# A fused attention, mixing and MLP block on one core: modulation sums in four column groups, V's low parts on another engine, later stores, and the mixing stage's first rows in a fixed buffer

## The chip, the core and the metric

The kernel runs on one core of a Trainium2 chip. The metric is device time in microseconds (us) of one execution, and lower is better. The engines named below are PE (TensorE: matmuls and transposes), DVE (VectorE), ACT (ScalarE), POOL (GpSimd) and SP (SyncE, which issues nearly all DMAs here). DRAM is the large memory outside the core. SBUF tiles live on 128 partitions, matmul results in eight PSUM banks of 128 x 512 fp32.

## The reference

One sequence of S = 2048 rows, D = 576 columns, F = 4608 hidden columns, 32 heads of 18 columns, everything fp32 in and out. The condition vector `c` (576) makes six vectors of 576 (shift, scale and gate for two branches). Cut to what matters:

```python
mod = silu(c) @ w_mod                     # six vectors: sa, ca, ga, sb, cb, gb
h   = layernorm(x) * (1 + ca) + sa
q, k, v = split(h @ wqkv)                 # 32 heads of 18
# every row attends to itself and the 255 rows before it
o   = softmax(q k^T * 18**-0.5, window 256) v @ wo
x   = x + ga * o
h   = layernorm(x) * (1 + cb) + sb        # the "hbd" rows
h2  = gelu(layernorm(h) @ w1)             # mixing: column groups shifted by +1, -1, +2, -2 rows
y   = h + shifted(h2) @ w2
z   = y + gelu(layernorm(y) @ w3) @ w4    # MLP
out = x + gb * z
```

## The kernel before

**Precision.** Nearly every 576-deep product is made of fp32r matmuls (a rounded fp32 format) on a high part and a low part of both operands, so that such a product of a 128-row by 512-column tile is 14 matmuls. Splitting an operand is a cast (high part) and a subtraction (low part), and the two run on ACT, POOL or DVE.

**Phase A** (`phase_a`, L189) is attention. Its work is a list `ev` of pairs (time, step). `play` sorts it and issues the steps in that order, and PE, DVE, ACT, POOL and SP keep the order in which they were issued. So the numbers in the list set the order of each engine, and each engine runs its row of instructions in order. The unit of time is a *unit*: 32 of them (four row blocks of 512 by eight groups of four heads), numbered 0 to 31. What happens before unit 0 has negative times and is called the head here.

**The head.** Some matmuls on zeros run first (`warm`, L264). `c_load` and `wm_load` bring `c` and the first third of `w_mod` (five pieces k = 0..4 of up to 128 rows by 1152 columns, L258). `cond` makes silu(c) and copies it to a tile `silub` of 128 x 640 in the ring of row buffers (tag "r", six of them). `mod_sum(k)` (L276) multiplies it by piece k with four fp32 matmuls of 128 rows by 256 or 320 columns, so that every PSUM partition holds the same sum; twenty instructions in all. `mod_col(j)` (L286) picks column j of the result to partitions by a multiplication with the identity, ten instructions on DVE. With `sa` and `ca` known, ACT makes `h` transposed (L373), POOL casts it to the high part of `hT` (L376), DVE makes the low part (L380). Then come the projections of block 0 (L391): an *item* is 14 matmuls, items 0, 4, 5, 1, 6, ... for Q and K (operand `Wc`), two per 128 rows for V (operand `Wv`). `Wv` is split per piece k: high part on ACT (L330), low part on POOL (L334).

**Packing.** Q and K go to DRAM and come back in the layout that the scores need: `pack(u)` (L457) issues twelve DMAs (L467 for Q, L469 for K) from SP. `scores(u)` (L483) takes 128-row maxima, `attend(u)` makes the scores again with the maxima subtracted (L530, L539), exponentials on ACT (L549, tile `P`), the products with V (L560, four column groups of 32), a transpose (L571), the quotient, and the store of the rows `o` to DRAM (`od`, L581).

**Output projection.** `s4a(t)` (L735) does it for row tile t of 128 rows, t = 0..11, within the last nine units. It loads the attention rows (`o`, L743) and the input rows (`x`, L747), transposes and splits the first, multiplies by `Wo` (L786) and adds into `x` (L791). At the same step it stores `x` to `xp` (L793). Then a layer norm writes `x` in place on ACT (L158), the modulation on POOL changes `x` in place and stores it to `hbd` (L803), and a second layer norm in place is followed by the store to `xnd` (L807).

**Mixing stage** (`phase_b`). Here the framework chooses the order. `s4` does tiles 12..15 of the output projection, `stage1` loads rows of `xnd` (L984), transposes and splits them to `xnT` (L98 to L106), `stage2` multiplies them by `W1` (L1017), with gelu on ACT, and so on. Then comes the MLP (`phase_c`).

**SP's queue.** SP issues its DMAs in order. Each DMA carries one of eight semaphores in turn (`DMAHW0` to `DMAHW7`), and waits for the DMA eight places before it, which the listings of order below show as `[waits DMAHWn...]`. So an SP instruction that waits for an engine holds back every DMA behind it.

Of the kernel before, what the change touches and what calls it, by code (L numbers as in the profile page):

```python
# [18 lines left out]
D = 576  # L19
F = 4608  # L20
P = 128
# [32 lines left out]
class Kern:  # L54
# [134 lines left out]
    def phase_a(self):  # L189
        nc = self.nc  # L190
        sm, gp, row = self.sm, self.gp, self.row
# [7 lines left out]
        with ExitStack() as st:  # L199
            ps = self.bank  # L200
            kv = self.pool(st, "kV")
            kp = self.pool(st, "kA")
            V = [kv.tile([P, H * VA + 13], F32, name=f"V{i}") for i in range(10)]
            Q = [kv.tile([P, 4, 512], F32R, name=f"Q{i}") for i in range(3)]
            K = [kv.tile([P, 2, 768], F32R, name=f"K{i}") for i in range(3)]
# [31 lines left out]
            def c_load():  # L237
                wm["c"] = ct = sm.tile([P, KC + 1], F32, name="ct", bufs=1)
                nc.vector.memset(ct, 0.0)
                nc.scalar.activation(silu[:, 0:1], ct[:, 0:1], AF.Exp)  # L240
# [4 lines left out]
            def cond():  # L245
# [5 lines left out]
                wm["s"] = gp.tile([P, KC + 1, P], F32, tag="r", name="silub", bufs=6)  # L251
                nc.vector.tensor_copy(wm["s"], silu.unsqueeze(2).to_broadcast([P, KC + 1, P]))
# [14 lines left out]
            half = ((0, 2 * P), (2 * P, D))  # L267

            def mod_sum(k):
                def f():  # L270
                    kk = P if k < KC else TAIL
                    for v in range(2):
                        for i, (c0, c1) in enumerate(half):
                            if k == 0:
                                wm[v, i] = ps([P, 512], ("sc", "st")[v], f"pms{v}{i}")
                            nc.tensor.matmul(wm[v, i][:, 0:c1 - c0], wm["s"][:kk, k, :], wm["t"][:kk, k, v * D + c0:v * D + c1], start=(k == 0), stop=(k == KC))  # L276
                return f

            def mod_col(j):
                def f():  # L280
                    n = P if j < KC else TAIL
                    i = j // 2 if j < KC else 1
                    c0 = j * P - half[i][0]
                    for v, dst in ((0, sa), (1, ca)):
                        pm = wm[v, i][:n, c0:c0 + n]
                        nc.vector.tensor_tensor_reduce(out=pm, in0=pm, in1=self.ident[:n, :n], scale=1.0, scalar=float(v), op0=ALU.mult, op1=ALU.add, accum_out=dst[:n, j:j + 1])  # L286
                return f
# [391 lines left out]
            for k in range(KC + 1):  # L679
                ev += v_split(k, -7.9 + 0.05 * k)  # L680
# [741 lines left out]
```

## Time and profile before

| what | us |
|---|---|
| three runs | 1730.81, 1741.58, 1737.53 |
| median | 1737.53 |
| the profiled execution, its own time | 1739.16 |
| its span, first to last instruction | 1737.4 |
| mean granted TensorE clock | 0.989 |
| PE busy | 1665.6 (96%) |

All moments below are microseconds from the start of that span. A row of the timeline has the moment, the duration of the run of equal instructions, the engine, the line, the operation with what it writes and reads, the count, and in brackets the idle time just before it and what ended it. A row of the windows has a stretch, its length, PE's busy time and count, the granted clock as a share of full speed, the DMA engines' share and GB/s. Matmuls in a row overlap a little, so a run is shorter than the sum of its parts.

### The profile page before, as it was taken

The page shows a single profiled execution, that of the slowest core. Times are in us where ns is not written, and L with a number is a line of the kernel's source. Part 1 is how long each engine was busy: PE and PEld are TensorE (multiplying, and loading weights), DVE is VectorE, ACT ScalarE, POOL GpSimd, SP SyncE. Part 2 cuts the span into 40 slices and gives each one's busy share as a digit, 9 for nine tenths or more (in the row PEclk, how much of TensorE's full clock was granted, in tenths as well). Part 3 has the DMA queues.
Part 4 walks back from the last instruction along what each step waited for, and adds up shares of the span by engine and source line. Part 5 has one row for each costly group of instructions (what it writes and reads, how often), then busy time and mean ns, then how long its engine had stood idle before and what let it go on. Part 6 is the DMA issues. An engine that isn't in the chain of part 4 may idle for free.

```text
span 1737.4 us, 30750 instructions
## 1 busy us (share of the span) xinstructions
PE 1665.6 (96%) x11100; PEld 1439.1 (83%) x11100; DVE 1172.6 (67%) x2543; ACT 700.9 (40%) x1310; POOL 812.6 (47%) x799
## 2 busy tenths in 40 slices
PE   7899999999999889999999999999999999999997
PEld 5777777877777777788989999999998999999997
DVE  3465566665567574777778888888876666666667
ACT  3254464554455555443243444343422222222221
POOL 6433141332225453044178888888864333332335
PEclk9999999999999899999999999999999999999999
DMA  5735544534557563653456555556665554445441
GB/s 167 201 122 150 150 128 134 155 107 125 137 154 197 154 195 110 203 158 103 162 182 219 210 201 187 186 206 221 216 217 166 168 165 146 143 137 168 156 150 68
DMA packets 161279, 283.33 MB, mean 163 GB/s; under 512 B 38500, under 2 KB 77412, under 8 KB 161128
## 3 DMA queue, kind: packets, MB, share of 16 engines
q1 hardware_dynamic: 158184, 275.54, 50.8%
q10 hardware_dynamic: 2944, 5.83, 1.2%
q8 instruction: 88, 1.44, 0.4%
q14 instruction: 63, 0.52, 0.1%
HBM read 168.86 MB, written 111.78 MB: 162 GB/s over the span
## 4 chain that ended last, share of the span: by engine, by line
PE 81%; DMA 6%; DVE 5%; POOL 3%; ACT 2%; issue 1%; SPq 1%; ACTq 0%; POOLq 0%; DVEq 0%
PE pall L1283 26%; PE pall L1329 22%; PE pall L391 8%; PE pall L560 4%; PE pall L530 4%; PE pall L483 4%; PE pall L1017 3%; PE pall L539 3%; PE pall L1068 2%; PE pall L786 2%; DVE pall L490 1%; DMA Q<-ms 1%; DMA wm<-in_w_mod_dram 1%; PE pall L276 1%; PE pall L571 1%
## 5 line engine op out<-in xcount | busy, mean ns | idle before, releaser
L1283 PE MATMUL pall<-LNT,W 128*128 128x512 f32 x2016 | 498.5, 390 | 1.9 <-ACT g L1287 1.9
L1329 PEld LDWEIGHTS pall<-W,G 128*128 128x128 f32 x3036 | 430.0, 189 | 25.9 <-DVE G L1249 4.3
L1329 PE MATMUL pall<-W,G 128*128 128x288 f32 x3036 | 443.4, 295 | 5.7 <-DVE G L1249 3.6
L1283 PEld LDWEIGHTS pall<-LNT,W 128*128 128x128 f32 x2016 | 365.7, 188 | 61.6 <-ACT g L1287 2.2
L490 DVE CUSTOM_DVE_ANT_0 pall<-pall,mask 128x384 f32<-128x384 f32 (+2 forms) x512 | 271.0, 543 | 209.2 <-PE pall L483 205.8
L1338 DVE TENSOR_TENSOR accA<-pall,accA 128x576 f32<-128x576 f32 x336 | 254.2, 757 | 127.3 <-PE pall L1329 115.2
L1254 POOL TENSOR_TENSOR g<-g,g 128x512 f32<-128x512 f32 x140 | 183.9, 1314 | 293.5 <-DVE G L1249 151.1
L549 ACT ACTIVATE P<-pall 128x512 f32<-128x512 f32 (+2 forms) x384 | 215.3, 570 | 166.0 <-PE pall L539 149.5
L1246 ACT CAST G<-g 128x512 fp32r<-128x512 f32 x249 | 151.0, 620 | 282.0 <-POOL g L1254 280.3
L1249 DVE TENSOR_TENSOR G<-g,G 128x512 fp32r<-128x512 f32 x249 | 241.5, 971 | 4.1 <-ACT G L1246 4.1
L483 PE MATMUL pall<-K,Q 108*128 108x384 f32 (+2 forms) x512 | 188.4, 379 | 13.5 <-DMA xnd<-s4rows 4.0
L530 PE MATMUL pall<-Q,K 110*128 110x384 f32 (+1 forms) x704 | 156.8, 297 | 16.7 <-ACT P L549 12.4
L1287 ACT ACTIVATE g<-pall 128x512 f32<-128x512 f32 x144 | 85.8, 596 | 201.7 <-PE pall L1283 192.1
L391 PE MATMUL pall<-hT,Wc 128*128 128x512 f32 x504 | 159.2, 415 | 3.4 <-ACT V L454 1.9
L1338 DVE TENSOR_TENSOR accB<-pall,accB 128x576 f32<-128x576 f32 x134 | 101.4, 757 | 89.8 <-PE pall L1329 87.7
L530 PEld LDWEIGHTS pall<-Q,K 110*128 110x128 f32 x704 | 125.1, 192 | 39.1 <-ACT P L549 20.9
L416 POOL CAST qe<-qe 128x512 fp32r<-128x512 f32 x36 | 22.6, 627 | 240.8 <-ACT qe L412 230.4
L539 PE MATMUL pall<-maskb,identb 128*128 128x256 bf16 (+1 forms) x640 | 121.4, 255 | 0.0
L483 PEld LDWEIGHTS pall<-K,Q 108*128 108x128 f32 x512 | 97.5, 195 | 21.4 <-issue 8.8
L391 PEld LDWEIGHTS pall<-hT,Wc 128*128 128x128 f32 x504 | 86.1, 192 | 17.3 <-issue 3.9
L391 PE MATMUL pall<-Wv,hT 128*128 128x288 f32 x448 | 85.0, 313 | 3.5 <-POOL Wv L334 2.4
L560 PE MATMUL pall<-P,V 128*32 128x384 f32 (+2 forms) x1408 | 86.9, 394 | 0.0
(651 smaller groups left out, 2076.9 us busy)
## 6 DMA issues: line engine op xcount, KB each, us to landing
w4d<-W SPq DMA_DIRECT2D x55, 576.0 KB
W<-w4d SPq DMA_DIRECT2D x55, 576.0 KB
w3d<-W SPq DMA_DIRECT2D x36, 640.0 KB
W<-w3d SPq DMA_DIRECT2D x36, 640.0 KB
K<-k0d SPq DMA_DIRECT2D x96, 108.0 KB
r<-in_B_w_dram SPq DMA_DIRECT2D x36, 288.0 KB
Q<-q0d SPq DMA_DIRECT2D x128, 72.0 KB
K<-k1d SPq DMA_DIRECT2D x48, 108.0 KB
```

The costliest lines, as they stand in the source:

```text
L391: nc.tensor.matmul(pm, pl()[i][0], pl()[i][1], start=(i == 0), stop=(i == 13))
L483: nc.tensor.matmul(sc[:, lo:], q[0:2 * R3, h, i * P:(i + 1) * P], k[0:2 * R3, h // 2, i * P + lo:(i + 3) * P], start=True, stop=True)
L490: nc.vector.tensor_tensor_reduce(out=sc[:, lo:], in0=sc[:, lo:], in1=mask[:, lo:], scale=1.0, scalar=-3e38, op0=ALU.add, op1=ALU.max, accu ...
L530: nc.tensor.matmul(x[:, p0 * P:(p0 + w) * P], k[0:2 * R3 + 2, h // 2, (kb + 2) * P:(kb + 3) * P], q[0:2 * R3 + 2, h, q0 * P:(q0 + w) * P], ...
L539: nc.tensor.matmul(x[:, p0 * P:(p0 + w) * P], self.identb, m, start=False, stop=(n == len(ms) - 1))
L549: nc.scalar.activation(pt[:, c0:c1, h % 2, :], x[:, c0 * P:c1 * P].rearrange("p (a b) -> p a b", b=P), AF.Exp, scale=SCALE)
L560: nc.tensor.matmul(abox[0][32 * h:32 * h + 32, q0 * P:(q0 + w) * P], v[:, hh * VA:hh * VA + 32], Pt[b, h // 2][:, p0:p0 + w, h % 2, :], st ...
L1249: nc.vector.tensor_tensor(out=sp[m][:, 1], in0=src(), in1=sp[m][:, 0].bitcast(F32), op=sub)
L1254: nc.gpsimd.tensor_tensor(out=g[o] if o in g else gt(o), in0=g[a], in1=g[b], op=op)
L1283: nc.tensor.matmul(box["p"], box["l"][i][1], box["l"][i][0], start=(i == 0), stop=(i == 13))
L1329: nc.tensor.matmul(po, a, b, start=(n == 0), stop=(n == len(seq) - 1))
L1338: nc.vector.tensor_tensor(out=acc2[m, i], in0=po, in1=acc2[m, i], op=ALU.add)
```

## The change

What it does, part by part:

1. **Modulation sums.** `silub` is 128 x 160 and leaves the row ring for another tag. `mod_sum(k)` issues four matmuls with 32 stationary columns and 320 moving ones, each to its own 32 PSUM partitions. A DVE copy of 128 x 320 (`mod_row`), three transposes (`mod_tr`) and four small DVE instructions (`mod_col`) replace the ten multiplications with the identity. The load of `c` comes a little earlier and no longer waits for ACT's first exponential.
2. **Weights and packing in the head.** `Wv`'s low parts go from POOL to DVE, as do the low part of `Wc` 0; V's splits get earlier times. `w_load(1)` comes after `v_load`. `pack(0)` is cut in two: Q's six DMAs first, K's six later. Item 6 comes whole before `scores(0)`.
3. **Output projection.** The stores to `od`, `xp`, `hbd`, `xnd` and `modd` become steps of their own at later times. Norm 1 writes into the buffer of the attention rows (`y`) instead of in place, the modulation works there, norm 2 writes from `y` back to `x`. The steps behind norm 1 come 0.04 to 0.11 units later.
4. **Mixing stage's first rows.** A fixed buffer `big` (128 x 4608 fp32r) takes the place of the third pair of Q and K tiles; when the last unit that uses them (29) is over, it becomes `xnT0`, and later every third `ltile`, so that the ring "L2" has two buffers instead of three. The loads of the rows 0..4 of `xnd`, the transposes and splits to `xnT0`, and three of the five W1 products of the first block (42 matmuls) get written times in units 29 to 31 (`xn_load`, `xnt0`, `w1_parts`). Their gelu stays in the mixing stage.

The order on PE in the head, around the sums (`wm` holds the pieces of `w_mod`, `x_...` are the four normed row tiles); before:

```order
L276 MATMUL pall<-wm,silub 128x256 [waits DMAHW1_49]
L276 MATMUL pall<-wm,silub 128x320
L276 MATMUL pall<-wm,silub 128x256
L276 MATMUL pall<-wm,silub 128x320
L276 MATMUL pall<-wm,silub 128x256 [waits DMAHW2_49]
L276 MATMUL pall<-wm,silub 128x320
L276 MATMUL pall<-wm,silub 128x256
L276 MATMUL pall<-wm,silub 128x320
L366 MATMUL pall<-ident,x_230 64x128 [waits Activation_49]
```

and now:

```order
L278 MATMUL pall<-wm,silub 32x320 [waits DMAHW1_49]
L278 MATMUL pall<-wm,silub 32x320 x3
L278 MATMUL pall<-wm,silub 32x320 [waits DMAHW2_49]
L278 MATMUL pall<-wm,silub 32x320 x3
L288 MATMUL pall<-ident,silub 128x128 [waits DVE_49]
L288 MATMUL pall<-ident,silub 128x128
L288 MATMUL pall<-ident,silub 64x128
L373 MATMUL pall<-ident,x_229 64x128
```

Pieces 3 and 4 still stand behind the transposes of x; each of their groups is four 32-column matmuls, and three transposes behind a wait for DVE stand before x's last transposes, which no longer wait for ACT.

V's low parts in the head (`Wv`, from the loaded rows `wvr`), with the casts of the Q and K items (`qe`). On POOL before:

```order
L416 CAST qe_0_421<-qe_0_421 128x512 [waits Activation_49]
L420 TENSOR_TENSOR qe_0_421<-qe_0_421 128x512 [waits Pool_49]
L334 TENSOR_TENSOR Wv<-wvr_388,Wv 128x576 [waits DMAHW2_49,DMAHW1_49,DMAHW6_49,DMAHW0_49,DMAHW7_49,PE_49,Activation_49]
L334 TENSOR_TENSOR Wv<-wvr_390,Wv 128x576 [waits DMAHW0_49,Activation_49]
L334 TENSOR_TENSOR Wv<-wvr_392,Wv 128x576 [waits DMAHW1_49,Activation_49]
L334 TENSOR_TENSOR Wv<-wvr_394,Wv 128x576 [waits DMAHW2_49,Activation_49]
L416 CAST qe_4_448<-qe_4_448 128x512 [waits Activation_49]
L334 TENSOR_TENSOR Wv<-wvr_396,Wv 128x576 [waits DMAHW4_49,DMAHW3_49,Activation_49]
L420 TENSOR_TENSOR qe_4_448<-qe_4_448 128x512 [waits Pool_49]
```

On DVE now (POOL's row has only the `qe` instructions there):

```order
L318 TENSOR_TENSOR Wc_293<-wr_292,Wc_293 128x512 [waits DMAHW1_49,Activation_49]
L319 TENSOR_TENSOR Wc_293<-wr_292,Wc_293 128x128 [waits DMAHW3_49,DMAHW2_49,Activation_49]
L341 TENSOR_TENSOR Wv<-wvr_380,Wv 128x576 [waits DMAHW4_49,Activation_49]
L341 TENSOR_TENSOR Wv<-wvr_382,Wv 128x576 [waits DMAHW5_49,Activation_49]
L341 TENSOR_TENSOR Wv<-wvr_384,Wv 128x576 [waits DMAHW6_49,Activation_49]
L341 TENSOR_TENSOR Wv<-wvr_386,Wv 128x576 [waits DMAHW7_49,Activation_49]
L341 TENSOR_TENSOR Wv<-wvr_388,Wv 128x576 [waits DMAHW1_49,DMAHW0_49,Activation_49]
```

The five subtractions left the queue in which the Q and K stores' casts stand, and follow the low parts of `Wc` on DVE.

SP's queue around the packing of unit 31 (`hbd`, `xp`, `xnd` are stores of the output projection, `xn` loads of the mixing stage). Before:

```order
L803 DMA hbd_88<-s4rows 128x576 [waits DMAHW4_49,Pool_49]
L984 DMA xn_7871<-xnd_98 128x576 [waits DMAHW5_49]
L984 DMA xn_7873<-xnd_99 128x576 [waits DMAHW6_49]
L984 DMA xn_7875<-xnd_100 128x576 [waits DMAHW7_49]
L984 DMA xn_7914<-xnd_101 128x576 [waits DMAHW0_49]
L984 DMA xn_7916<-xnd_102 128x576 [waits DMAHW1_49,Pool_49]
L793 DMA xp_121<-s4rows 128x576 [waits DMAHW2_49,DVE_49]
L467 DMA Q_170<-q0d_143 18x2x512 [waits DMAHW3_49,PE_49]
L469 DMA K_173<-k0d_151 18x2x768 [waits DMAHW4_49,PE_49]
```

Now:

```order
L823 DMA s4rows<-in_A_x_dram 128x576 [waits DMAHW0_49]
L879 DMA xnd_103<-s4rows 128x576 [waits DMAHW1_49,Activation_49]
L879 DMA hbd_88<-s4rows 128x576 [waits DMAHW3_49,Pool_49]
L475 DMA Q_171<-q0d_143 18x2x512 [waits DMAHW4_49,PE_49]
L478 DMA K_173<-k0d_151 18x2x768 [waits DMAHW5_49,PE_49]
L475 DMA Q_171<-q1d_144 18x2x512 [waits DMAHW6_49]
```

The five loads of `xn` and the store of `xp` stood between the `hbd` store and the packing, and now stand behind it. SP issues 1175 DMA rows in both kernels.

The diff, cut to its core:

```diff
-            Q = [kv.tile([P, 4, 512], F32R, name=f"Q{i}") for i in range(3)]
-            K = [kv.tile([P, 2, 768], F32R, name=f"K{i}") for i in range(3)]
+            Q = [kv.tile([P, 4, 512], F32R, name=f"Q{i}") for i in range(2)]
+            K = [kv.tile([P, 2, 768], F32R, name=f"K{i}") for i in range(2)]
+            Q.append(big[:, 0:2048].rearrange("p (a b) -> p a b", a=4))
+            K.append(big[:, 2048:3584].rearrange("p (a b) -> p a b", a=2))
...
-                            nc.tensor.matmul(wm[v, i][:, 0:c1 - c0], wm["s"][:kk, k, :], wm["t"][:kk, k, v * D + c0:v * D + c1], start=(k == 0), stop=(k == KC))
+                    for q, (v, c0) in enumerate((v, c0) for v in range(2) for c0 in (0, 2 * P)):
+                        nc.tensor.matmul(wm["p"][32 * q:32 * q + 32, :], wm["s"][:kk, k, :], wm["t"][:kk, k, v * D + c0:v * D + c0 + 320], start=(k == 0), stop=(k == KC))
...
+            def mod_row():
+                nc.vector.tensor_copy(wm["r"], wm["p"])
+
+            def mod_tr():
+                wm["q"] = ps([P, 3, P], "sc", "pmt")
+                for j in range(3):
+                    n = P if j < 2 else TAIL
+                    nc.tensor.transpose(wm["q"][:n, j, :], wm["r"][:, j * P:j * P + n], self.ident)
...
-                    nc.gpsimd.tensor_tensor(out=w[:, l, :], in0=Wv["r", k], in1=w[:, h, :].bitcast(F32), op=ALU.subtract)
+                    nc.vector.tensor_tensor(out=w[:, l, :], in0=Wv["r", k], in1=w[:, h, :].bitcast(F32), op=ALU.subtract)
...
+                if u == 0:
+                    ev += [(-7.6, pack(0, ks=False)), (-7.3, pack(0, qs=False))]
...
+            for t in range(5):
+                ev += [(w1 + 7.4 + 0.1 * t, self.xn_load(t))]
+            for t in range(4):
+                ev += self.xnt0(t, NB * NU - 0.9 + 0.2 * t)
+            for fc, t in ((KC, -0.1), (0, 0.2), (1, 0.565)):
+                ev += spread(self.w1_parts(0, fc), NB * NU + t, NB * NU + t + 0.3)
...
-                if hf == 1:
-                    nc.sync.dma_start(self.xp[t], x)
...
-        b2, r2, n2, g2 = self.stat_steps(x, f"c{t}")
+        b2, r2, n2, g2 = self.stat_steps(y, f"c{t}")
...
-        e += [(0.86, b1), (0.89, r1), (1.06, n1), (1.08, lambda: self.norm(x(), x(), g1())), (1.14, mod)]
-        e += [(1.42, b2), (1.45, r2), (1.6, n2), (1.62, ln2)]
+        e += [(0.86, b1), (0.88, keep(self.xp, x)), (0.89, r1), (1.06, n1), (1.13, lambda: self.norm(y(), x(), g1())), (1.19, mod)]
+        e += [(1.46, keep(self.hbd, y)), (1.46, b2), (1.49, r2), (1.66, n2), (1.73, lambda: self.norm(x(), y(), g2())), (1.86, keep(self.xnd, x))]
```

156 lines of the change are left out of this document (101 added, 55 removed).

## The prediction

> **What bounds the kernel now.** I read the page first, then the windows by stage, the timeline of PE with its idle times, and for each long idle time the timeline of the engine or queue named in it.
>
> ```profile
> PE 1665.6 (96%) x11100; PEld 1439.1 (83%) x11100; DVE 1172.6 (67%) x2543; ACT 700.9 (40%) x1310; POOL 812.6 (47%) x799
> PE 81%; DMA 6%; DVE 5%; POOL 3%; ACT 2%; issue 1%; SPq 1%; ACTq 0%; POOLq 0%; DVEq 0%
> ```
>
> ```profile
> 0.00:80.00 80.00, 66.12 (x310) 0.94 0.65 179
> 80.00:480.00 400.00, 384.40 (x3072) 0.99 0.48 135
> 500.00:700.00 200.00, 175.96 (x1522) 0.97 0.61 168
> 700.00:880.00 180.00, 173.47 (x1070) 1.00 0.49 157
> 880.00:1200.00 320.00, 320.00 (x1884) 1.00 0.58 199
> ```
>
> PE bounds the program, and in the MLP (880 to 1200) it never idles. So time can be gained only where PE idles, runs at a low clock, or does work that goes away. That is 13.9 us of idle time in the head (80 minus 66.12) and 24.0 us between 500 and 700 (200 minus 175.96). The change touches just these two stretches. The middle (80 to 480) keeps its order nearly row by row, and I give it nothing.
>
> **The head, part 1 and 2.** PE's rows of the head, then three rows of ACT, DVE and POOL, and one of SP:
>
> ```profile
> 11.75 7.75 PE L276 MATMUL pall<-wm,silub 128*128 128x256 f32 x24 [3.14 <-DMA wm<-in_w_mod_dram]
> ...
> 21.09 4.24 PE L276 MATMUL pall<-wm,silub 128*128 128x256 f32 x16
> ...
> 31.83 7.13 PE L391 MATMUL pall<-hT,Wc 128*128 128x512 f32 x30 [0.60 <-DVE hT L380]
> 38.79 1.48 PE L391 MATMUL pall<-Wv,hT 128*128 128x288 f32 x10
> 40.95 0.67 PE L391 MATMUL pall<-Wv,hT 128*128 128x288 f32 x3 [0.68 <-POOL Wv L334]
> 43.37 3.71 PE L391 MATMUL pall<-Wv,hT 128*128 128x288 f32 x15 [1.75 <-POOL Wv L334]
> 47.57 3.47 PE L391 MATMUL pall<-hT,Wc 128*128 128x512 f32 x14 [0.49 <-ACT V L454]
> 50.87 3.86 PE L391 MATMUL pall<-Wv,hT 128*128 128x288 f32 x28
> ...
> 59.96 0.30 PE L483 MATMUL pall<-K,Q 108*128 108x128 f32 x1 [2.60 <-DMA K<-k1d]
> 60.09 2.70 PE L391 MATMUL pall<-hT,Wc 128*128 128x512 f32 x6
> 62.58 1.64 PE L483 MATMUL pall<-K,Q 108*128 108x128 f32 x6
> ```
>
> ```profile
> 25.22 2.79 ACT L373 ACTIVATE h<-pall,sa,ca 128x512 f32<-128x512 f32 x4 [5.14 <-DVE ca L286]
> ```
>
> ```profile
> 31.81 0.69 DVE L311 TENSOR_TENSOR Wc<-wr,Wc 128x512 fp32r<-128x512 f32 x1
> ...
> 40.17 1.27 DVE L311 TENSOR_TENSOR Wc<-wr,Wc 128x512 fp32r<-128x512 f32 x1 [6.67 <-ACT Wc L306]
> ```
>
> ```profile
> 35.32 5.58 POOL L334 TENSOR_TENSOR Wv<-wvr,Wv 128x576 fp32r<-128x576 f32 x4
> ```
>
> ```profile
> 18.55 0.47 SPq L116 DMA_DIRECT2D wr<-in_A_wqkv_dram  x1
> ```
>
> Everything in the head hangs on `h`, which starts at 25.22, when the sums are over (21.09 + 4.24 = 25.33, a little later even). The sums' data are there earlier: SP's issue at 18.55 uses the semaphore of the last piece of `w_mod`, so that piece had landed by then. How long the new sums take, the attention's own products in four column groups show:
>
> ```profile
> 691.43 2.80 PE L560 MATMUL pall<-P,V 128*32 128x384 f32 x48
> ```
>
> In these 48 matmuls each of the four groups streams 12 tiles of 128 columns, 1536 in all, and 2.80 us / 1536 is 1.82 ns per column with all four at work. A piece is 320 columns in each of four groups: 0.58 us, against 12.0 us / 5 = 2.4 us now. The last piece is summed at 18.55 + 0.58 = 19.1. Behind it come the copy of 128 x 320 on DVE, three transposes and four small DVE instructions, none of them in the trace in this form. With the 0.69 us DVE row as the upper bound of the copy, and some 0.2 us for each of the rest, that is 0.5 to 2 us, and I take 1.6. So `h` starts at 20.7, **4.5 us earlier**, and the Q and K items with it (38.79 becomes 34.3).
>
> V's items suffer from POOL: two items of 28 matmuls take from 38.79 to 47.08 where the same 28 take 3.86 us at 50.87. POOL needs 5.58 / 4 = 1.40 us for a low part, between the casts of the Q and K items that it holds up. DVE idles there (6.67 us before 40.17) and does a subtraction of nearly this size in 0.69 to 1.27 us. So V's items cost 3.9 instead of 8.3: 34.3 + 0.3 + 3.9 = 38.5, 8.6 us earlier than 47.1. Then 47.57's item, V's next two and the whole of item 6 follow: 3.5 + 3.9 + 3.4 us and some 0.9 us between, to 50.2. The trace now has the scores of unit 0 at 62.58, behind 2.60 us of waiting for K's packing and 2.70 us for six matmuls that should take 1.4. If Q and K are packed by 50, the head has gained 12 us there. POOL's queue is 7 us shorter before the casts of the K items, and Q's half of the packing no longer stands behind K's, so the packing should begin 8 to 10 us sooner, which is about two less than PE would like. I take **-11**. The bounds are -4.5 (only the sums help, and the rest waits for DMAs) and -14 (all the idle time of the head gone).
>
> **Output projection, part 3, and the packing of unit 31.** The long idle times of PE between 500 and 700, with what they waited for on ACT and SP, and the granted clock behind two of them:
>
> ```profile
> 583.81 0.79 PE L530 MATMUL pall<-Q,K 110*128 110x384 f32 x2 [3.60 <-ACT P L549]
> ...
> 595.02 0.50 PE L530 MATMUL pall<-Q,K 110*128 110x384 f32 x2 [2.03 <-ACT P L549]
> ...
> 653.24 0.41 PE L483 MATMUL pall<-K,Q 108*128 108x384 f32 x1 [4.02 <-DMA xnd<-s4rows]
> ```
>
> ```profile
> 582.41 0.87 ACT L158 ACTIVATE s4rows<-s4rows,b4rs 128x576 f32<-128x576 f32 x1 [4.94 <-DMA xp<-s4rows]
> ...
> 593.62 0.87 ACT L158 ACTIVATE s4rows<-s4rows,c4rs 128x576 f32<-128x576 f32 x1 [1.45 <-DVE c4rs L143]
> ```
>
> ```profile
> 635.15 0.32 SPq L803 DMA_DIRECT2D hbd<-s4rows  x1
> 635.52 2.35 SPq L984 DMA_DIRECT2D xn<-xnd  x5
> 637.97 0.38 SPq L793 DMA_DIRECT2D xp<-s4rows  x1
> 638.44 0.30 SPq L467 DMA_DIRECT2D Q<-q0d  x1
> ```
>
> ```profile
> 584.00:586.00 2.00, 2.00 (x9) 0.50 0.25 93
> ...
> 655.00:657.00 2.00, 2.00 (x12) 0.50 0.45 158
> ```
>
> At 582.41 ACT's norm had waited 4.94 us until the store of the same rows to `xp` had been read out, because it writes in place; the exponentials stood behind it, and PE behind them. The new norm 1 writes to `y`, whose earlier reader (the transposes) is long done, so this wait goes: -3.6. Norm 2 now overwrites `x` and so waits for the `xp` store, but 0.85 units after it instead of 0.2. The wait of 1.45 us at 593.62 is for the statistics, and these steps moved 0.05 units apart (about 1 us): -1.0 of 2.03. The packing of unit 31 loses the six DMAs ahead of it (638.44 minus 635.52 is 2.9 us of issue), while the `hbd` store ahead of both may come up to 1 us later: -3.0 of 4.02. Each stall left PE at half clock, which costs 1.0 us per 2 us stretch; two of these go: -2.0. Sum **-9.6**, and the bounds are -3.6 (the first alone) and 3.60 + 2.03 + 4.02 + 2.0 = -11.7. What is late next is the `xnd` store, a fraction of a unit later, whose reader (the loads of `xn`) also moved back.
>
> **Mixing stage's first rows, part 4.** PE idles in and behind unit 31, as the windows of unit 31's attention and of what follows it show, and then a row of each of PE and SP:
>
> ```profile
> 680.00:691.00 11.00, 9.44 (x96) 1.00 0.26 92
> 691.00:707.00 16.00, 12.57 (x98) 1.00 0.71 207
> ```
>
> ```profile
> 694.16 0.66 PE L98 MATMUL pall<-ident,xn 128*128 128x128 f32 x4
> ...
> 706.75 0.63 PE L98 MATMUL pall<-ident,or 128*128 128x128 f32 x4 [1.55 <-DMA or<-od]
> ```
>
> Of the 42 matmuls of W1, 28 now stand before the last products of unit 31; at 7.13 / 30 = 0.24 us that is 6.7 us of work. PE has 11 - 9.44 = 1.6 us idle there, waiting for exponentials, so the products end some 5 us later. Behind them the store of the last `o` and its load as `or` take 12.6 us (694.16 to 706.75), whatever PE does. In that stretch PE does 27 matmuls of W1 before the change and 25 after it, so 26 more of them lie behind it when `or` comes: -6.2 + 5.0, and a little for the transposes that now fill waits: **-1.5**. The bounds are -5.0 (all the idle time of both windows, 1.6 and 3.4) and 0, if the eight copies to `xnT0` on ACT hold up the exponentials.
>
> **The rivals.**
>
> *The head stays bound by DMAs.* For it: the DMA share of 0.65 over the head, and 2.60 us of wait for `K<-k1d`. Against it: these DMAs waited for POOL's casts. Then the head gives -4.5 instead of -11, and the time is 1739.2 - 4.5 - 9.6 - 1.5 = 1723.6. It would come to the same if the column groups ran one after another: 4 x 0.58 us is what the sums take now.
>
> *The stalls of 500 to 700 only move.* SP's queue still carries every store, and a store that waits holds the packings behind it. Then that stretch gives -2: 1739.2 - 11 - 2 - 1.5 = 1724.7. Against it: each store now comes when its rows are ready.
>
> *Slower.* The later stores could land ahead of a packing in SP's queue in most units. The `hbd` store at 635.15 shows how: it waited for POOL, with a packing behind it, and PE stood 4.02 us, and 1.0 us went to the clock. Nine packings (units 23 to 31) lie beside the output projection. From five such stalls of 5.0 us the gain of 22 us is gone; with all nine the time is 1739.2 - 22 + 45 = 1762.
>
> *A low clock in the head.* Shorter sums between landings leave PE idle before the Q and K items. A stall of 3.60 us was followed by a granted clock of 0.50; two such stretches of 2 us would cost 2.0 us, and the time is 1739.2 - 22.1 + 2.0 = 1719.1. [...]
>
> **How the numbers follow.** The sum is -11 - 9.6 - 1.5 = -22.1 against the profiled execution of 1739.2 us, 1717.1. That execution lies 1.6 us above the median of the three runs (1737.5), so against the median it is 1715.5, and I say 1715. Chances: the forecast 0.55, the low clock 0.12, the head bound by DMAs 0.12, stalls that move 0.12, slower 0.09. About 1% (17 us) is what a measurement of this kernel can tell from no change, so faster means below 1720: forecast and low clock, 0.67. Within 1% come the two rivals in which half the gain fails, 0.24, and slower has 0.09. The range goes from all bounds at their best (-14, -11.7, -5: 1708) a little down to 1706, and up to both middle rivals at once (-4.5, -2, -1.5), 1731.
>
> **What would show it.** In the changed kernel's profile `h` (ACT, now L380) should start near 21, the second V item end near 39, and the scores of unit 0 stand near 50. No norm of the output projection should wait for a store to `xp`, and no stall of 3 us should be left in 500 to 700, nor a granted clock of 0.5 there. PE should have less idle time before the first `or` transposes relative to its W1 work. The prediction is wrong if the packing of unit 0 ends late, or if SP's row shows a store waiting ahead of packings.

## The result and the profile after

The changed kernel takes 1722.89 us in the median (1718.01 to 1726.02, four runs), and the kernel before 1737.59 us (1730.81 to 1741.58, four runs). The ratio is 0.9915 with a 95% interval of 0.989 to 0.994. That is 14.7 us less, 0.85%: a gain clear of noise, inside the range of the prediction, but two thirds of the 22 us forecast, and under the 1% to which 0.67 of the chances had been given. The profiled execution has a span of 1721.5 us, 15.9 less than the one before.

The page of the changed kernel, busy time and the windows by stage, in the same columns as before:

```profile
PE 1658.1 (96%) x11103; PEld 1434.0 (83%) x11103; DVE 1178.9 (68%) x2535; ACT 701.5 (41%) x1310; POOL 805.2 (47%) x792
```

```profile
0.00:80.00 80.00, 69.57 (x381) 0.94 0.68 200
80.00:480.00 400.00, 385.73 (x3074) 0.99 0.48 135
500.00:700.00 200.00, 181.84 (x1561) 0.98 0.63 174
700.00:880.00 180.00, 172.69 (x1066) 0.99 0.48 156
880.00:1200.00 320.00, 320.00 (x1883) 1.00 0.59 200
```

In the last row PE is as full in the MLP as it was. The stretch 500 to 700 has 18.2 us of idle time instead of 24.0, although the stalls that the prediction named are gone. So something new idles there.

Where time was won and lost is read best from the moments at which the two executions reach the same instruction. The table is worked out from the traces (the second of the sixteen matmuls of each unit's scores; the first of an operation elsewhere). The lead is before minus after; the last column is the lead in a second profiled execution of the changed kernel, taken for the experiments on another chip.

| reached | before, us | after, us | lead, us | lead in the second profile |
|---|---|---|---|---|
| scores of unit 0 | 62.58 | 47.34 | 15.2 | 12.9 |
| scores of unit 2 | 88.11 | 76.80 | 11.3 | 8.2 |
| scores of unit 23 | 484.45 | 472.71 | 11.7 | 11.0 |
| scores of unit 25 | 522.89 | 513.52 | 9.4 | 10.0 |
| scores of unit 30 | 631.56 | 611.52 | 20.0 | 21.9 |
| scores of unit 31 | 655.11 | 630.29 | 24.8 | 26.7 |
| last of unit 31's products with V | 693.85 | 676.15 | 17.7 | 19.7 |
| first matmul of the MLP | 862.86 | 846.89 | 16.0 | 20.5 |
| last product of the MLP | 1733.02 | 1717.15 | 15.9 | 18.8 |

Two gains are there, about as large as forecast or larger: 11 us by unit 2, and 15 us between units 25 and 31. Then 9 us (6 in the second profile) are lost between unit 31's scores and the MLP, where the prediction had put a gain of 1.5.

**The head after.** PE, ACT, and the last DMA of unit 0's packing on SP, before the change and now:

```profile
15.37 1.62 PE L278 MATMUL pall<-wm,silub 128*32 128x320 f32 x16
...
25.19 7.14 PE L398 MATMUL pall<-hT,Wc 128*128 128x512 f32 x30 [0.38 <-DVE hT L387]
32.16 3.87 PE L398 MATMUL pall<-Wv,hT 128*128 128x288 f32 x28
35.87 3.36 PE L398 MATMUL pall<-hT,Wc 128*128 128x512 f32 x14
39.06 3.87 PE L398 MATMUL pall<-Wv,hT 128*128 128x288 f32 x28
42.77 3.36 PE L398 MATMUL pall<-hT,Wc 128*128 128x512 f32 x14
47.20 0.54 PE L492 MATMUL pall<-K,Q 108*128 108x128 f32 x3 [1.08 <-DMA wr<-in_A_wqkv_dram]
...
58.41 0.44 PE L492 MATMUL pall<-K,Q 108*128 108x128 f32 x1 [3.51 <-DMA wr<-in_A_wqkv_dram]
```

```profile
18.57 2.79 ACT L380 ACTIVATE h<-pall,sa,ca 128x512 f32<-128x512 f32 x4 [0.73 <-DVE ca L294]
```

```profile
54.96 0.27 SPq L469 DMA_DIRECT2D K<-k1d  x1
43.28 0.27 SPq L478 DMA_DIRECT2D K<-k1d  x1
```

`h` starts at 18.57 (20.95 in the second profile). From 25 to 46 PE runs item after item with no wait for POOL. The packing of unit 0 is issued 11.7 us sooner. The next thing that is late is unit 1: 3.51 us ahead of its scores. The bracket names a load of `wr`, but these matmuls read only `Q` and `K`, and experiment 9 takes the wait away by moving their packing.

**The output projection after.** Norm 1 of tile 4 (the one that waited 4.94 us before) on ACT, and SP around the packing of unit 31:

```profile
570.66 0.86 ACT L158 ACTIVATE s4rows<-s4rows,b4rs 128x576 f32<-128x576 f32 x1
579.96 0.87 ACT L158 ACTIVATE s4rows<-s4rows,c4rs 128x576 f32<-128x576 f32 x1 [0.55 <-DVE c4rs L143]
```

```profile
615.17 0.32 SPq L879 DMA_DIRECT2D hbd<-s4rows  x1
615.58 0.30 SPq L475 DMA_DIRECT2D Q<-q0d  x1
```

The norm waits for nothing any more, and norm 2 waits 0.55 us for its statistics where it waited 1.45. The packing follows the `hbd` store at once. How much the stalls cost is read from the stretch between unit 27's scores and unit 30's, in which two of the three lay, before and now:

```profile
563.08:631.56 68.48, 59.68 (x492) 0.93 0.63 170
554.05:611.52 57.47, 54.79 (x493) 1.00 0.76 212
```

The stretch is 11.0 us shorter. PE's idle time falls from 8.8 us to 2.7, which is 6.1 us, and a granted clock of 0.93 over 68.48 us is worth another 4.8 us.

**Behind unit 31.** PE's rows, and the windows:

```profile
673.74 2.80 PE L569 MATMUL pall<-P,V 128*32 128x384 f32 x48
676.46 1.65 PE L799 MATMUL pall<-big,W 128*128 128x512 f32 x6
677.95 0.60 PE L580 MATMUL pall<-ident,avs 128*128 128x128 f32 x4
678.31 2.10 PE L799 MATMUL pall<-big,W 128*128 128x512 f32 x8
680.25 0.60 PE L98 MATMUL pall<-ident,xn 128*128 128x128 f32 x4
680.68 0.27 PE L104 MATMUL pall<-ident,xn 128*64 128x128 f32 x1
682.62 0.66 PE L98 MATMUL pall<-ident,xn 128*128 128x128 f32 x4 [1.66 <-DVE xnT L106]
683.93 1.66 PE L799 MATMUL pall<-big,W 128*128 128x512 f32 x6 [0.65 <-ACT gf L1092]
685.42 0.27 PE L104 MATMUL pall<-ident,xn 128*64 128x128 f32 x1
685.45 1.41 PE L799 MATMUL pall<-big,W 128*128 128x512 f32 x5
690.86 1.09 PE L98 MATMUL pall<-ident,or 128*128 128x128 f32 x4 [4.01 <-DMA or<-od]
```

```profile
680.00:691.00 11.00, 4.68 (x24) 0.92 0.72 201
691.00:705.00 14.00, 14.00 (x77) 0.82 0.40 117
```

Of the 11 us from 680 to 691 PE works 4.68. It has three waits in a row: for the splits of `xnT`, for the first gelu, and for `or`, the rows that come back from DRAM. And then it works at a lowered clock, 0.82 over 14 us, which is 2.5 us more.

### The profile page after: what moved, and what is told of

It is laid out like the page before. It is cut to its first block, busy times and chain, and to the rows that moved or that the text cites. A ratio compares the mean times of both kernels' runs of the same rounds, so it can differ in the third digit from the quotient of the medians.

```text
span 1721.5 us, 30735 instructions
## 1 busy us (share of the span) xinstructions
PE 1658.1 (96%) x11103; PEld 1434.0 (83%) x11103; DVE 1178.9 (68%) x2535; ACT 701.5 (41%) x1310; POOL 805.2 (47%) x792
## 4 chain that ended last, share of the span: by engine, by line
PE 52%; DVE 1%; POOL 1%; issue 0%; DMA 0%; ACT 0%; POOLq 0%; DVEq 0%
PE pall L1358 26%; PE pall L1404 23%; PE pall L1141 2%; PE pall L799 2%; POOL accA L1419 1%; DVE accA L1419 0%; DVE G L1324 0%; PE pall L98 0%; DVE accA L1413 0%; DMA r<-in_B_w_dram 0%; POOL c L1251 0%; POOL x L1160 0%; POOL x L1161 0%; DVE xm L160 0%; DVE accB L1413 0%
## 5 line engine op out<-in xcount | busy, mean ns | idle before, releaser
L1404 PEld LDWEIGHTS pall<-W,G 128*128 128x128 f32 x3036 | 431.3, 189 | 24.5 <-DVE G L1324 2.8
L1358 PE MATMUL pall<-LNT,W 128*128 128x512 f32 x1512 | 375.3, 390 | 1.9 <-ACT g L1362 1.9
L1358 PEld LDWEIGHTS pall<-LNT,W 128*128 128x128 f32 x1512 | 274.8, 188 | 47.7 <-ACT g L1362 2.2
L492 PE MATMUL pall<-K,Q 108*128 108x384 f32 (+2 forms) x352 | 128.6, 378 | 9.6 <-DMA wr<-in_A_wqkv_dram 4.6
L1358 PE MATMUL pall<-big,W 128*128 128x512 f32 x504 | 126.2, 390 | 0.0
L539 PE MATMUL pall<-Q,K 110*128 110x384 f32 (+1 forms) x480 | 105.5, 293 | 6.8 <-ACT P L558 4.7
L1358 PEld LDWEIGHTS pall<-big,W 128*128 128x128 f32 x504 | 90.9, 188 | 14.1
L539 PEld LDWEIGHTS pall<-Q,K 110*128 110x128 f32 x480 | 84.6, 190 | 21.6 <-ACT P L558 8.2
```

Of the source, the lines that this page charges most:

```text
L492: nc.tensor.matmul(sc[:, lo:], q[0:2 * R3, h, i * P:(i + 1) * P], k[0:2 * R3, h // 2, i * P + lo:(i + 3) * P], start=True, stop=True)
L539: nc.tensor.matmul(x[:, p0 * P:(p0 + w) * P], k[0:2 * R3 + 2, h // 2, (kb + 2) * P:(kb + 3) * P], q[0:2 * R3 + 2, h, q0 * P:(q0 + w) * P], ...
L1358: nc.tensor.matmul(box["p"], box["l"][i][1], box["l"][i][0], start=(i == 0), stop=(i == 13))
L1404: nc.tensor.matmul(po, a, b, start=(n == 0), stop=(n == len(seq) - 1))
```

## The experiments

All ratios are to the kernel before, run on the same chip in the same job; "lead" is that of the table above. Each kernel is the changed one with the edit shown.

**1. The W1 products behind unit 31.**

```diff
-            for fc, t in ((KC, -0.1), (0, 0.2), (1, 0.565)):
+            for fc, t in ((KC, 0.565), (0, 0.87), (1, 1.18)):
```

> The changed kernel, with the 42 W1 matmuls of the first block written behind unit 31's last products instead of 28 of them ahead. Theory (the work put ahead of unit 31 only takes away cover): the last products end about 5 us earlier against unit 31's scores (6.7 us of matmuls less 1.6 us of waits that they filled), the 6.3 us of idle time ahead of the or transposes shrink to under 2, and the time is about 5 us below the changed kernel's, near 1718 (20 us below before). Rival (tiles 12 to 15 and the gelus behind them set the end whatever PE did before): within 2 us of the changed kernel, 1721 to 1725.

Measured: 1718.95 us, ratio 0.9894 (0.9877 to 0.991). The lead at unit 31's scores is 24.5 us, as in the changed kernel; 20.5 at the end of its products (17.7 there), 22.3 at the MLP (16.0). PE behind unit 31:

```profile
670.75 3.02 PE L569 MATMUL pall<-P,V 128*32 128x384 f32 x48
673.70 1.66 PE L799 MATMUL pall<-big,W 128*128 128x512 f32 x6
675.19 0.60 PE L580 MATMUL pall<-ident,avs 128*128 128x128 f32 x4
675.54 8.45 PE L799 MATMUL pall<-big,W 128*128 128x512 f32 x36
683.83 0.60 PE L98 MATMUL pall<-ident,xn 128*128 128x128 f32 x4
684.27 0.27 PE L104 MATMUL pall<-ident,xn 128*64 128x128 f32 x1
684.30 2.52 PE L799 MATMUL pall<-big,W 128*128 128x512 f32 x10
687.31 0.63 PE L98 MATMUL pall<-ident,or 128*128 128x128 f32 x4 [0.50 <-DMA xr<-in_A_x_dram]
```

The wait of 4.01 us ahead of the `or` transposes is 0.50, and the others ahead of it are gone: 52 matmuls of W1 stand there now, where 25 stood, and fill the time in which the last `o` goes to DRAM and comes back. Unit 31's last products come 3.1 us earlier against its scores, where 5 had been expected. The theory holds in the trace, with that size too high. In the medians it is worth 4 us, by ratios whose intervals overlap.

**2. Part 4's first rows back in the mixing stage.** The loads, `xnt0` and `w1_parts` are taken out of the list, and the mixing stage does block 0 as before:

```diff
-            for t in range(5):
-                ev += [(w1 + 7.4 + 0.1 * t, self.xn_load(t))]
-            for t in range(4):
-                ev += self.xnt0(t, NB * NU - 0.9 + 0.2 * t)
-            for fc, t in ((KC, -0.1), (0, 0.2), (1, 0.565)):
-                ev += spread(self.w1_parts(0, fc), NB * NU + t, NB * NU + t + 0.3)
...
-                if g == 0:
-                    continue
```

> The changed kernel with the first rows' transposes, splits and W1 products left to the mixing stage as before; the fixed buffer stays. Theory (part 4 cost time): 3 to 6 us below the changed kernel, like the kernel with the W1 products written behind unit 31. Rival (part 4 gained the 1.5 us of the prediction, and what was lost was lost for another reason): 1 to 3 us above the changed kernel.

Measured: 1722.16 us, ratio 0.9913 (0.9898 to 0.9927): no difference from the changed kernel that these runs show. Neither theory's number came. In the trace the lead falls from 20.7 us at unit 31's scores to 15.8 at the MLP, a loss of 4.9. The changed kernel's two profiles lose 8.9 and 6.2 there, the kernels of experiments 3 to 8, which leave part 4 as it is, 5.1 to 7.1, and experiment 1's loses 2.2. So part 4 as written cost between nothing and 4 us in this stretch, and its work put in the right place won some 3.

Up to the last of unit 31's products with V this kernel loses 4.0 us, and so does experiment 1's, though no W1 product stands ahead of them in either. PE idles 4.0 us in unit 31 here and 4.7 in experiment 1, against 2.1 before the change, mostly for exponentials (2.6 and 3.1 us against 1.6), and works at a granted clock of 0.66 from 667 to 677 us here and of 0.79 from 664 to 672 there (before, 0.50 from 655 to 657). Why the exponentials are later against unit 31's scores was not tried. So of the 7.1 us that the changed kernel loses up to these products, the 28 W1 products ahead of them cost 3.1.

**3. The sums in full width.** `mod_sum` and `mod_col` as before, `silub` in its new tag:

```diff
-                wm["s"], wm["r"] = box[:, 0:160].rearrange("p (k m) -> p k m", m=32), box[:, 160:480]
+                wm["s"] = gp.tile([P, KC + 1, P], F32, tag="oT", name="silub", bufs=1)
...
-            ev += [(-8.9, mod_row), (-8.89, mod_tr), (-8.885, mod_col)]
+            ev += [(-8.85 + 0.01 * j, mod_col(j)) for j in range(KC + 1)]
```

> The changed kernel with the modulation sums back in 20 matmuls of 128 stationary columns and the ten multiplications with the identity. Theory (the head hangs on h): h starts near 25 instead of 18.6, the scores of unit 0 come 6 us later, and the time is 5 to 7 us above the changed kernel. Rival (the head is bound by its DMAs and the packing): the scores of unit 0 come at most 2 us later, and the time is within 2 us of the changed kernel.

Measured: 1723.71 us, ratio 0.993 (0.9915 to 0.9945): 2.6 us above by the ratios, which the intervals do not tell from nothing. `h` starts at 21.00, not near 25, and unit 0's scores come at 50.05, so the theory's 6 us did not come; the changed kernel's own two profiles (47.34 and 49.66) lie too far apart to say more of the rival. The sums start without a stall:

```profile
9.22 6.06 PE L280 MATMUL pall<-wm,silub 128*128 128x256 f32 x24
15.12 1.91 PE L370 MATMUL pall<-ident,x 128*128 128x128 f32 x16
16.86 4.24 PE L280 MATMUL pall<-wm,silub 128*128 128x256 f32 x16
```

They ended at 25.33 before the change and end at 21.10 here, 4.2 us earlier: 2.5 by the earlier start (9.22 against 11.75), and 1.7 because they take 11.9 us instead of 13.6. The second part is the granted clock, which differs from one profile to the next (windows of 20 us):

| kernel | `h` starts, us | clock, 0 to 20 | clock, 20 to 40 |
|---|---|---|---|
| before | 25.22 | 0.91 | 1.00 |
| changed, first profile | 18.57 | 1.00 | 0.91 |
| changed, second profile | 20.95 | 0.83 | 0.91 |
| sums in full width | 21.00 | 1.00 | 0.91 |
| experiment 9's kernel, run again (experiment 11) | 19.48 | 0.91 | 0.91 |
| the same, sums in full width (experiment 12) | 23.69 | 0.91 | 0.83 |

With the same clock over the first 20 us, the narrow sums bring `h` 2.4 us sooner (at 1.00) or 4.2 (at 0.91). So the earlier start and the narrow form both count, and only the comparison at one clock tells them apart.

**4. V's low parts on POOL.**

```diff
-                    nc.vector.tensor_tensor(out=w[:, l, :], in0=Wv["r", k], in1=w[:, h, :].bitcast(F32), op=ALU.subtract)
+                    nc.gpsimd.tensor_tensor(out=w[:, l, :], in0=Wv["r", k], in1=w[:, h, :].bitcast(F32), op=ALU.subtract)
```

> The changed kernel with V's five low parts back on POOL. Theory (after the sums the head is PE's row of items, and POOL's 1.4 us per low part with the casts of the Q and K items held them up): waits for POOL return among V's items, K's packing of unit 0 begins 5 us or more later, the scores of unit 0 come 4 to 7 us later, and the time is 3 to 6 us above the changed kernel. Rival (K's packing and the DMAs set unit 0 anyway): the scores of unit 0 within 2 us, and the time within 2 us.

Measured: 1727.88 us, ratio 0.9935 (0.9913 to 0.9958), 3.5 us above by the ratios. In the trace `h` starts at 19.58, and then the old waits return:

```profile
35.76 0.66 PE L398 MATMUL pall<-Wv,hT 128*128 128x288 f32 x3 [0.71 <-POOL Wv L341]
38.18 2.90 PE L398 MATMUL pall<-Wv,hT 128*128 128x288 f32 x15 [1.76 <-POOL Wv L341]
65.86 0.45 PE L492 MATMUL pall<-K,Q 108*128 108x128 f32 x1 [4.91 <-DMA wr<-in_A_wqkv_dram]
```

The lead is 9.2 us at unit 0 and 4.1 at unit 2, where the changed kernel's two profiles have 11.3 and 8.2. The lead at unit 2 is below that of all eight profiles with the changed kernel's head (6.8 to 11.3). The theory holds.

**5. Norms in place and stores at their producers.** `s4a` as before the change:

```diff
-        b2, r2, n2, g2 = self.stat_steps(y, f"c{t}")
+        b2, r2, n2, g2 = self.stat_steps(x, f"c{t}")
...
-        e += [(0.86, b1), (0.88, keep(self.xp, x)), (0.89, r1), (1.06, n1), (1.13, lambda: self.norm(y(), x(), g1())), (1.19, mod)]
+        e += [(0.86, b1), (0.89, r1), (1.06, n1), (1.08, lambda: self.norm(x(), x(), g1())), (1.14, mod)]
```

> The changed kernel with the output projection's steps as before: norms in place, each store at its producer's step. The loads of xn and the packing of unit 31 keep their new order. Theory (the in-place norm's wait for the xp store stalls PE): a stall of 3 to 4 us near unit 26 returns with a half clock behind it, and the time is 6 to 9 us above the changed kernel. Rival (the gain between units 25 and 31 comes from the new place of the xn loads alone): within 3 us of the changed kernel.

Measured: 1735.91 us, ratio 0.9988 (0.9974 to 1.0001): 13 us above, nearly all that the whole change had won, and more than either theory said. ACT's norm again waits 4.88 us for the `xp` store, and PE's stalls are back as they were:

```profile
582.96 0.80 PE L539 MATMUL pall<-big 110*128 110x384 f32 x2 [3.51 <-ACT P L558]
594.11 0.50 PE L539 MATMUL pall<-Q,K 110*128 110x384 f32 x2 [2.04 <-ACT P L558]
```

**6. Only the stores back at their producers.**

```diff
-(0.88, keep(self.xp, x))
+(0.776, keep(self.xp, x))
...
-(1.46, keep(self.hbd, y)), (1.46, b2)
+(1.1901, keep(self.hbd, y)), (1.46, b2)
...
-(1.86, keep(self.xnd, x))
+(1.7301, keep(self.xnd, x))
```

> The changed kernel with each store of the output projection back right behind its producer (xp, hbd, xnd), while the norms still write to the other buffer. Theory (part 3's gain is the other buffer, which takes away the wait for the xp store): within 3 us of the changed kernel. Rival (part 3's gain is that the stores no longer wait at the head of SP's queue): most of the 13 us that undoing part 3 cost, so 6 us or more above the changed kernel.

Measured: 1728.74 us, ratio 0.9931 (0.9904 to 0.9958), 2.8 us above by the ratios. That is just within the theory's 3 us and far from the rival's 6; the intervals overlap with the changed kernel's.

**7 and 8. The loads of `xn` ahead of the `hbd` store, and between it and the packing.** Experiment 7, then 8:

```diff
-                ev += [(w1 + 7.4 + 0.1 * t, self.xn_load(t))]
+                ev += [(w1 + 6.2 + 0.05 * t, self.xn_load(t))]
...
+                ev += [(w1 + 6.632 + 0.005 * t, self.xn_load(t))]
```

> The changed kernel with the five loads of xn 1.2 units earlier, ahead of the hbd store and the packing of unit 31 as before the change. Theory (the 2.9 us of issue ahead of the packing caused the stall of 4.0 us): unit 31's scores come 3 to 5 us later against unit 30's, and the time is 2 to 5 us above the changed kernel. Rival (the packing was late because of the norms ahead of the hbd store): unit 31's scores within 1.5 us, and the time within 2 us.

Measured: 1720.8 us, ratio 0.9897 (0.9871 to 0.9924): no slower. But these loads went out while SP waited for the `hbd` store anyway, and behind that store there was nothing, so this did not test what stood there before. Hence the next:

> The changed kernel with the five loads of xn between the hbd store and the packing of unit 31, where they stood before the change; the run with the loads ahead of the hbd store put them into a time in which SP waited anyway. Theory (issue between that store and the packing delays unit 31): the packing begins 2.4 us later behind the hbd store, unit 31's scores come 2 to 4 us later against unit 30's than in the changed kernel, and the time is 2 to 4 us above it. Rival (the packing's own pace was what the norms delayed): unit 31's scores within 1 us against unit 30's.

Measured: 1728.93 us, ratio 0.9952 (0.9934 to 0.9969), 6.4 us above by the ratios. SP's queue, then PE:

```profile
618.13 0.32 SPq L879 DMA_DIRECT2D hbd<-s4rows  x1
618.50 2.34 SPq L757 DMA_DIRECT2D xn<-xnd  x5
620.94 0.30 SPq L475 DMA_DIRECT2D Q<-q0d  x1
```

```profile
635.72 0.66 PE L492 MATMUL pall<-K,Q 108*128 108x384 f32 x1 [3.59 <-DMA xp<-s4rows]
```

Again the bracket names a store, while the row reads `Q` and `K`. The packing's twelve DMAs are issued in 10.3 us (620.94 to 631.2) instead of 5.6 (615.58 to 621.2). SP's waits from 618 to 632 us show why:

```profile
SPq L475 <- DMA xn<-xnd: 3.1, 2, 3.0
SPq L478 <- DMA xn<-xnd: 2.5, 2, 1.6
```

Each row has the total, the number and the longest of the waits. A DMA on SP waits for the one eight places before it (the semaphores `DMAHW0` to `DMAHW7` in the listing of order), so four DMAs of the packing waited 5.6 us until the loads had landed. In the changed kernel's profile no packing DMA of unit 31 waits for `xn`; before the change they waited 2.6 us for it. The lead does not grow between unit 30's scores and unit 31's, so the theory holds, with a price above the one expected. What experiments 5 to 8 say about parts of the output projection stands in one table of how much lead is won:

| kernel | units 25 to 30, us | units 30 to 31, us |
|---|---|---|
| changed, first profile | 10.7 | 4.8 |
| changed, second profile | 11.9 | 4.8 |
| norms in place, stores at producers | -2.7 | 3.0 |
| other buffer, stores at producers | 8.0 | 3.8 |
| `xn` loads ahead of the `hbd` store | 10.8 | 4.7 |
| `xn` loads between it and the packing | 12.0 | -0.2 |

The other buffer, together with the later norm steps that experiment 5 also takes back, is worth some 11 us, the later stores some 4, and the place of the `xn` loads the whole 5 us of the last column.

**9. The packing of unit 1 sooner,** on the kernel of experiment 1:

```diff
-            ev += [(-7.4, lambda: clear(1)), (-7.35, lambda: clear(2)), (-1.2, vones(4, 10))]
+            ev += [(-7.4, lambda: clear(1)), (-1.25, lambda: clear(2)), (-1.2, vones(4, 10))]
...
-            wt = {0: -8.975, 4: -8.974, 5: -8.973, 1: -8.7, 6: -7.45, 2: -1.9, 7: -1.5, 3: -1.2, 8: -0.9}
+            wt = {0: -8.975, 4: -8.974, 5: -8.973, 1: -8.7, 6: -7.45, 2: -1.9, 7: -1.45, 3: -1.2, 8: -0.9}
```

> The kernel with the W1 products behind unit 31, and with POOL's clearing of the third Q and K pair put behind item 1's split, and the load of the weights of item 7 put behind the packing of unit 1 on SP. Theory (the 3.5 to 5 us stall ahead of unit 1's scores is the packing of unit 1, which stands behind 3.2 us of clearing on POOL and 1.7 us of issue on SP): the stall falls below 1 us, the half clock behind it goes, and the time is 3 to 6 us below that kernel, near 1714. Rival (the stall is the DMA engines' own pace): the stall stays over 2.5 us, and the time is within 2 us of that kernel.

Measured: 1714.15 us, ratio 0.9853 (0.9823 to 0.9883). No idle time of over 0.5 us is left ahead of unit 1's scores, and the lead at unit 2 is 14.7 us. By the ratios it is 7 us below experiment 1's kernel, more than expected, but the two ran on different chips. The edit does two things, POOL's clearing and the place of one load on SP, and which of them counts was not separated.

**10 to 12. Three kernels on one chip, five rounds each.** The changed kernel, the kernel of experiment 9, and the latter with the sums of experiment 3:

> The changed kernel itself, beside the next two on one chip. Both theories: 14 to 16 us below before.

> The kernel with the W1 products behind unit 31 and the packing of unit 1 sooner, once more beside the changed kernel. By the two earlier comparisons: 8 to 11 us below the changed kernel, 24 to 26 below before.

> The same kernel with the modulation sums back in full width, in the version in which no packing stall stands behind the head. Theory (the sums' new form is worth the 2.4 us by which h starts sooner, 18.6 against 21.0): the scores of unit 0 and the time 2 to 3 us above the kernel with the narrow sums. Rival (a packing stall behind it hides it again): within 1 us, with a stall of unit 0's or unit 1's packing shorter by as much as h is later.

| kernel | median, us | ratio and interval | `h` starts, us | lead at unit 0 | lead at unit 2 |
|---|---|---|---|---|---|
| changed | 1722.11 | 0.9913 (0.9889 to 0.9937) | 20.95 | 12.9 | 8.2 |
| W1 behind, packing sooner | 1715.56 | 0.9878 (0.9854 to 0.9902) | 19.48 | 14.7 | 13.3 |
| the same, sums in full width | 1714.32 | 0.9869 (0.9843 to 0.9895) | 23.69 | 8.9 | 9.0 |

The kernel of experiment 9 is 6.6 us below the changed kernel here, less than expected, and in this execution 2.35 us of the stall ahead of unit 1 were left. Each of its six runs here (1713.69 to 1718.51) is below each of the changed kernel's (1720.36 to 1723.95), so it beats both kernels. The sums in full width make no difference that the times show (-1.2 us, intervals nearly alike), though in the profiles `h` starts 4.2 us later and the lead at unit 2 is 4.2 us smaller. The 2.35 us ahead of unit 1 are not there with the sums in full width, so the rival's hidden stall is part of it. The expected 2 to 3 us are neither shown nor ruled out.

## Why the prediction was right, and where its sizes were wrong

The direction and the range held, and so did the mechanism of the two main gains. The sum came to 15.9 us in the profile through two errors that partly cancel. The median of 1722.9 lies next to the 1723.6 and 1724.7 of the two middle rivals, but what they say did not happen in the head or in units 25 to 31; that the numbers meet is chance.

- **The head, -11 predicted.** 11.7 us by unit 23 in one profile, 11.0 in the other. Right in size, and half right in its reasons. "`h` starts at 20.7" was met (18.57 and 20.95), the V items at 34 to 38 were met (32.16 to 36.03), and experiment 4 shows that POOL's low parts were the hold-up. But the step "4.5 us earlier" was put down to the short sums alone. It came to 6.7 us in one profile and 4.3 in the other, and experiment 3 shows two more causes: the sums start up to 2.5 us sooner, and the clock over them differs from profile to profile. The new sums measured 1.62 / 2 = 0.81 us per piece, where the products with V had given 0.58.
- **What is late next.** The prediction named K's packing of unit 0. It was the packing of unit 1, with 3.51 us; experiment 9 removed it in one profile and cut it in the other.
- **The output projection, -9.6 predicted.** From unit 23 to 31 the lead grew by 13.1 us, from unit 25 by 15.4 (and by 15.7 and 16.7 in the second profile). The waits that were named went, as predicted, but two terms were too small. The low clock behind the stalls, -2.0, was read from two stretches of 2 us; between units 27 and 30 it is worth 4.8 us. The idle time, -3.6 and -1.0, is 6.1 us there. Undoing the buffer and the store times cost 13 us of time and 15 of lead between units 25 and 31, and brought back a clock of 0.93 and 9.2 us of idle time over units 27 to 30. Whether ACT's wait also slowed POOL and the stores of the units around it was not tried. The term for the packing of unit 31, -3.0 for the issue ahead of it, was 5 us (experiment 8), since the packing also had to wait until those loads had landed.
- **The first rows, -1.5 predicted.** This step failed. It came out at a loss of 8.9 us (6.2 in the second profile) between unit 31's scores and the MLP. Not all of that is part 4's: experiment 2, without its work, loses 4.9 us there. The prediction had it that the store and load of the last `o` take 12.6 us "whatever PE does", and that 25 matmuls would stand there to cover them. Both were in the rows. What it counted wrongly is the cover: those 25 take 6 us, 12.6 us were to be filled, and eleven of them had to wait themselves, for splits and for a gelu. PE stood idle 6.3 of 11 us, and the low clock behind that cost 2.5 more. Twenty-eight matmuls had been moved to a place where only 1.6 us of idle time waited for them; they cost 3.1 us there, not 5. Experiment 1 puts them behind, and the loss falls to 2.2.
- **The rivals.** Bound by DMAs: no, the head won 11 us, and experiment 4 gives part of it back by POOL alone. Stalls that only move in 500 to 700: not within the units, yes at their end. Slower through SP's queue: the mechanism is real (experiment 8: 5 us for one misplaced group of loads), but the change removed a case of it and did not add one. A low clock in the head: it came, at about its price. From 20 to 24 us the granted clock is 0.57, and twelve matmuls of the first Q and K items take 4.73 us where thirty take 7.14 behind them; that is 1.7 us (4 x 0.43), and the second profile has a clock of 0.91 over 20 to 40 us as well, where it was 1.00 before. The mean of the first 80 us stays at 0.94 because before the change the clock was low elsewhere, in the sums among others (0.57 from 12 to 16 us). The idle time between the sums does not stand right ahead of it, though: among the narrow sums PE works 3.94 of the 6 us from 8 to 14, and 2.00 of the 2 us from 14 to 16, at a clock of 1.00 in both. What stands ahead of the low clock in this profile is the wait behind the sums (0.58 us of work from 18 to 20).
- **The signs.** `h`, the V items and unit 0's scores came near their places or sooner, and no norm waits for an `xp` store. Three signs went the other way. In 500 to 700 a stall of 4.01 us and a clock of 0.50 (691 to 695) are left, PE idles more ahead of `or` instead of less, and the `hbd` store still waits 4.3 us for POOL with unit 31's packing behind it. The last one costs PE little: it idles 0.5 us between unit 30's scores and unit 31's.

The head's lead at unit 2 scatters between 6.8 and 11.3 us in eight profiles of kernels with the same head. A good part of that is the clock: it is 0.87 over the first 80 us in the profile with 6.8, and 0.94 in the one with 11.3. What stays open is why the clock differs there, and whether the narrow sums are worth anything in the time. A loss of 1 to 4 us of lead around units 24 to 26, in nearly all profiles of the changed kernel and its variants, was seen and not tried.

## What to carry to other kernels

Before moving work out of a stretch, ask what it covers there: filler that stands behind a store and a load has its use, and the time it fills must be counted against the time that is open at its new place. A stall's price is not its idle row alone: here the lowered clock behind the stalls cost nearly as much again (4.8 us between units 27 and 30, beside 6.1 us of idle time), and the lead at equal instructions, unit by unit, shows the whole of it. When a group of DMAs is put into an in-order queue, its place counts: the same five loads cost nothing that the runs show ahead of a store that waited anyway (ratio 0.9897, the changed kernel's 0.9915), and some 6 us (0.9952) right ahead of a packing that then had to wait for them. And where two profiles differ in the granted clock, their moments can't be compared without it: `h` of the same kernel started at 18.57 us where the clock over the first 20 us was 1.00, and at 20.95 where it was 0.83.

## What the runs showed of the hardware that was not expected

- Five loads of 128 x 576 between one store and a packing of twelve DMAs took 2.34 us of issue, and the packing then ran from 620.94 to 631.2, 10.3 us, against 5.6 us without them (615.58 to 621.2). The two delays add, and the second is waiting: 5.6 us until the loads had landed, in a queue where each DMA waits for the one eight places before it.
- Equal head code reached unit 2's scores at moments up to 4.5 us apart from one profiled execution to another, while the lead then stays equal to within 0.2 us for many units (units 9 to 18 in the first profile: 11.7 to 11.9). In the eight profiles with the changed kernel's head (its own two and those of experiments 1, 2 and 5 to 8) `h` starts at 18.57 us where the granted clock over the first 20 us is 1.00, at 19.28 and 19.74 where it is 0.91, and at 20.95 to 21.57 where it is 0.83. A difference of a few microseconds in the head can't be judged by one execution.
